# A recurrence feeding a routed expert layer: where a small input check and the first zeroings stand

## The chip, the cores and the metric

The kernel runs on one core of one Trainium2 chip, as one launch. The metric is device time in microseconds (us), the median of several executions. Engines are named as the profile names them: PE (matrix products), DVE, ACT, POOL, and SP, which here only issues DMAs.

## What is computed

Three stages follow each other. The first is a recurrence over 768 tokens for 32 heads (4 batches of 8) with a 40 by 40 state each; the other two are a layer of eight experts, of which every token takes two, and a dense layer.

```python
for t in range(S):                       # S = 768, per batch and head, D = 40
    y[:, :, t] = einsum('bhd,bhde->bhe', rt, state)
    Sa = einsum('bhde,bhe->bhd', state, at)
    state = state * wt[:, :, None, :] - einsum('bhd,bhe->bhde', Sa, bt) + einsum('bhd,bhe->bhde', vt, kt)
...
x = y.transpose(0, 2, 1, 3).reshape(3072, 320)
noisy = x @ w_gate + log1p(exp(x @ w_noise)) * noise      # top 2 of 8 experts, softmax over the two
out[mask] += weight * (relu(x[mask] @ w1[e]) @ w2[e])     # for every expert e and both places
h = out @ w_in; result = maximum(0.01 * h, h) @ w_out
```

## The kernel before

The 768 tokens are cut into 12 chunks of 64 (`NCH`). For each chunk there is a preparation, which needs only inputs, and a chain of steps through the state. The preparation is `load` and `load_w` (DMAs of k with b, of a twice, and of the decays w), `wq` (two scans over the decays, `Dt` and `Et`, for each half q of the heads, their transposes on PE, and the products of k, b and a with them), `sta` and `stk_` (16-bit stacks, transposed by DMA), `ks` (scores on PE) and the steps of a small triangular inverse (`t_load`, `t_step`, `t_fin`). The chain is `c_x`, `c_u`, `c_s`; the outputs are `y_u` to `y_t`, and after each chunk the router's logits are formed. When chunk 11 is near, `Moe.setup` builds the router's constants, `Moe.route` and `Moe.routed` sort the tokens to the experts, and then `moe1` and `moe2` run the two layers.

`Attn.run` gives every step a due number with `at(k, f)`, sorts the steps by it and calls them in that order; the extra steps of the router are in `A.extra` with due numbers of their own. The framework then orders each engine's instructions by its own simulation of the program, so that a moved step can move others with it. Tiles come from pools on two sides of the on-chip memory. A pool that is closed gives its room to later tiles, and the first instruction that writes such a tile waits for the last one that used the room.

What stands at the program's start before: `consts` zeroes the state `S` (L41) and four tiles `x` (L44) on POOL, builds index tiles with `iota` (L47 to L60) and from them masks on DVE (L48 to L62). `body` then takes a pool named `ck`, loads 120 KB of all six inputs (the tile `cx`) by ACT's queue, and finds on DVE whether any of the six is small throughout (L795 to L797, result in `bad`). `Attn.run` opens the pools of the chunks' tiles, which fall on the room of `ck` and of the index tiles, and zeroes on POOL `cd` and `ce` (the scans' second operands), the rows of five tiles `aT` that no load fills, `VU`, `T` and `TT` (all L235). The chunks' loads follow, in the order k with b, a, and so on by chunk (SP's queue is one queue, kept in order). Chunks 0 and 1 have due numbers far below the others.

The second scan of chunk 0, `Et` for q=1, overwrites the only buffer of `Et`, so that it must wait until POOL has multiplied `aT` by the first `Et` (L93).

Of the kernel before, what the change touches and what calls it, by code (L numbers as in the profile page):

```python
# [7 lines left out]
F32 = mybir.dt.float32  # L8
# [10 lines left out]
# head 8g+4f+i is kept as (f, z=4g+i); on the state's rows as (z%2, z//2)  # L19
def host_attn(r,k,v,w,a,b):  # L20
    n=lambda y: np.ascontiguousarray(y.reshape(B,2,4,NCH,C,D).transpose(3,1,4,0,2,5).reshape(NCH,2,C,16*D))       # c f t (z e)
    t=lambda y: np.ascontiguousarray(y.reshape(B,2,2,2,NCH,C,D).transpose(4,3,6,0,2,1,5).reshape(NCH,2,D,16,C))   # c z%2 e (z/2 f) t
    k,b=n(k),n(b); wt=t(w); wz=np.ones((NCH,2,2,64,8,C),np.float32); wz[:,:,:,:D]=wt.reshape(NCH,2,D,2,8,C).transpose(0,3,1,2,4,5); wz[...,0]=0
    wz=np.pad(wz.reshape(NCH,2,128,8*C)[:,:,:104],((0,0),(0,0),(0,0),(1,1)))   # c q (z%2 e) (z/2 f t), without the chunk's first, 0 on both sides
    first=lambda wt: np.ascontiguousarray(np.pad(wt[...,0].transpose(1,2,0,3),((0,0),(0,24),(0,0),(0,0)),constant_values=1).reshape(128,NCH*16)[:104])
    return dict(kb=np.ascontiguousarray(np.stack([np.concatenate([k[:,0],b[:,0]],1),np.concatenate([b[:,1],k[:,1]],1)],1)),
        aa=n(a).reshape(NCH,128,640),rr=n(r).reshape(NCH,128,640),vv=n(v).reshape(NCH,128,640),at=t(a).reshape(NCH,2,D,1024),
        wz=wz,w0=first(wt))

class Attn:  # L30
# [7 lines left out]
    def consts(s,tp):  # L38
        nc=s.nc; cp=s.cp; V=nc.vector; G=nc.gpsimd;
        # state, rows (z%2, e): the first 64 rows' alone, the last 64 rows' alone, all rows'  # L40
        s.S=cp.tile([128,16,120],F32,name="S"); G.memset(s.S,0.0)  # L41
        s.ss=cp.tile([128,16,128],F16,name="ss"); V.memset(s.ss,0.0)
        s.x=[cp.tile([128,4,2,40],F32,name=f"x{i}") for i in range(4)]   # row half f holds f's
        for t in s.x: G.memset(t,0.0)  # L44
        s.VU=[cp.tile([128,2,16,40],F32,name=f"VU{i}") for i in range(2)]
        jp=tp.tile([128,128],I32,name="jp")
        G.iota(jp,pattern=[[1,128]],base=0,channel_multiplier=-1)   # col-row  # L47
        s.idf=cp.tile([128,128],F32,name="idf"); V.tensor_scalar(s.idf,jp,0.0,None,op0=ALU.is_equal)  # L48
        # earlier tokens: of the scores, and of k, b with a (b's rows of the first half against the second half's a)
        s.masky=cp.tile([128,64],F32,name="masky"); s.mask=[cp.tile([128,64],F32,name=f"mask{f}") for f in range(2)]  # L50
        for i in range(2): V.tensor_scalar(s.masky[64*i:64*i+64],jp[64*i:64*i+64,64*i:64*i+64],0.0,2.0**-6,op0=ALU.is_gt,op1=ALU.mult)
        cb=tp.tile([128,64],I32,name="cb"); k=4; nb=4   # nb + col>>k - row>>k
# [8 lines left out]
        s.gap=cp.tile([128,1],F32,name="gap"); t1=tp.tile([128,1],F32,name="t1")   # 0 on the rows between  # L61
        V.tensor_scalar(t1,pr,64.0,2.0**-12,op0=ALU.is_ge,op1=ALU.mult); V.tensor_scalar(s.gap,pr,40.0,2.0**-12,op0=ALU.is_lt,op1=ALU.mult); V.tensor_tensor(s.gap,s.gap,t1,ALU.add)  # L62
        
    # ---- loads of chunk c
    def load_w(s,c,q):
        w=s.K['w',c,q]=s.wp.tile([104,514],F32,name="w",bufs=s.cfg['bw']); s.nc.sync.dma_start(out=w,in_=s.h['wz'][c,q])
    def load(s,c):
        nc=s.nc; K=s.K[c]=dict(); aT=s.aT[c%s.cfg['NA']]
        K['en']=s.st.tile([128,16,40],F32,name="en",bufs=s.cfg['NE']); K['aa']=s.wp.tile([128,16,40],F32,name="aa",bufs=1); K['kb']=[]
        for f in range(2):  # L70
            kb=s.st.tile([128,16,40],F32,name="kb",bufs=s.cfg['NK']); K['kb'].append(kb)
            nc.sync.dma_start(out=kb.rearrange("p a b->p (a b)"),in_=s.h['kb'][c,f])
        nc.sync.dma_start(out=K['aa'].rearrange("p a b->p (a b)"),in_=s.h['aa'][c])
        for p in range(2): nc.sync.dma_start(out=aT[64*p:64*p+40].rearrange("p a b->p (a b)"),in_=s.h['at'][c,p])
    # ---- decays of z 8q..8q+7, and k, b, a with them
    def wq(s,c,q):
# [9 lines left out]
        V.tensor_scalar(w0,W4,2.0**-12,None,op0=ALU.mult)   # the chunk's decay in its first token's place  # L86
# [13 lines left out]
    # rows h,h,l (or h,l,h) of x in a stack, and its transpose  # L100
# [17 lines left out]
    def psx(s,c):   # two banks, [128,4,128] and [128,512]  # L118
        a,b='ys','yy'; f=lambda n,*d: s.ps.tile([128,*d],F32,name=n,bufs=1)
        x=f(a,4,128) if a=='pt' else f(a,8,64).rearrange("p a b->p (a b)").rearrange("p (a b)->p a b",b=128)  # L120
        return x,(f(b,512) if b=='yy' else f(b,8,64).rearrange("p a b->p (a b)"))
# [13 lines left out]
    # ---- T of the diagonal blocks of a group of chunks (two): 32 rows a partition, (chunk, f, z, block)  # L135
# [5 lines left out]
    def blk(s,c,t,off,*d):   # of both blocks of 16  # L141
# [11 lines left out]
    # ---- r, v of chunk c  # L153
# [8 lines left out]
    # ---- chain: heads (f, 4g..4g+3), tokens 32 blk + 16 h..  # L162
# [32 lines left out]
    # ---- y  # L195
    def y_u(s,c,h):   # v's and u's stack of half the heads
# [26 lines left out]
    def y_d(s,c):   # state for the y of chunk c  # L223
# [7 lines left out]
    def run(s):  # L231
# [5 lines left out]
        s.cd=s.wp.tile([104,8,64],F32,name="cd"); s.ce=s.wp.tile([104,8,64],F32,name="ce")  # L237
        zero(s.cd); zero(s.ce); V.memset(s.cd[:,:,63:64],4096.0)
        s.aT=[s.st.tile([128,16,64],F32,name=f"aT{i}") for i in range(F['NA'])]
        for t in s.aT: zero(t[32:64]); zero(t[96:128])  # L240
# [4 lines left out]
        for t in s.VU: zero(t)  # L245
        s.T=s.wk.tile([128,32,32],F32,name="T",bufs=1); zero(s.T)
        s.N=s.wk.tile([128,32,32],F32,name="N",bufs=1); s.tm=s.wk.tile([128,272],F32,name="tmp",bufs=1)
        s.TT=[s.st.tile([128,48,32],F32,name=f"TT{i}") for i in range(2)]; s.nT=0   # k of the first half, zeros, k of the second half
        for t in s.TT: zero(t[:,16:32])
# [7 lines left out]
        last=NCH-1; PC=cf.get('pc',5); dg=PC/4; base=lambda c: PC*c; tl=cf.get('tp',1.)  # L257
        pb=cf.get('pb',0); base=lambda c: PC*c+pb*((c+o)//2); ke=-99
        la=cf.get('la',2.6)   # prep of chunk c goes with the chain of chunk c-la
# [27 lines left out]
RND=6; R=4            # rounds of R token tiles of 128: rows b*768+128*q of round q  # L287
PT=124; NJ=7; CAP=PT*NJ   # slots of an expert: slot p*NJ+j

def tails(w):   # [320,n] -> [128,3,n]: the rows 256.. twice  # L290
    return np.ascontiguousarray(np.stack([w[0:128],w[128:256],np.concatenate([w[256:320],w[256:320]],0)],1))
def gates(w):   # [320,16] -> [128,2,80]: of heads' halves f the first 128 rows; the last 32 rows of batch b's on rows 32b.., columns 16+16b..
# [5 lines left out]
def host_moe(w_gate,w_noise,noise,w1,w2,w_in,w_out):  # L298
    return dict(wgs=gates(np.concatenate([w_gate,w_noise],1)),wg=tails(np.concatenate([w_gate,w_noise],1)),
        noise=np.ascontiguousarray(noise.reshape(4,RND,128,NE).transpose(2,3,1,0)),   # [p, e, round, b]  # L300
# [6 lines left out]
class Moe:  # L307
# [4 lines left out]
    # power of two scale: absmax in [2^k,2^(k+1)) and its inverse; bits worked on in int32 by float arithmetic on exponents  # L312
# [10 lines left out]
    # ---- what routing keeps  # L323
# [10 lines left out]
    def setup0(s,wgs):   # what the logits need  # L334
# [3 lines left out]
    # logits of chunk c: x rows (f, token), [b, 160]  # L338
# [10 lines left out]
    def absmax0(s,z,t):   # part z of the first expert's weights, into t [128,1024]  # L349
# [6 lines left out]
    def setup(s,rk):  # L356
        nc=s.nc; cp=s.P("mcst"); s.rk=rk(); V=nc.vector; G=nc.gpsimd
        with s.tc.tile_pool(name="mtmp",bufs=1) as tp:
# [6 lines left out]
            s.ei=s.rk.tile([128,NE,NTL],F32,name="ei"); G.iota(s.ei,pattern=[[-1,NE],[0,NTL]],base=NE,channel_multiplier=0,allow_small_or_imprecise_dtypes=True)  # 8-e  # L365
# [8 lines left out]
    # am [128,n] -> out [128,2n]: scales, inverses (of the maximum over all partitions)  # L374
# [11 lines left out]
    # exp to float32's accuracy: 2^n exp(f), |f|<=ln2/2; z is lost  # L386
# [15 lines left out]
    # ---- routing of round q: x rows [128,R,320]  # L402
    def big(s): return [s.ra.tile([128,16,40],F32,name="kb",bufs=s.rb).rearrange("p a b->p (a b)") for i in range(2)]
    def direct(s,c,xt):   # rows of chunk c right to where its round is routed
# [24 lines left out]
    def routed(s,q0,q1,nm,E=None,B_=None,A_=None):   # what follows for rounds q0..  # L429
# [10 lines left out]
        # log1p(exp(z)): one step of Newton's from the tables' value  # L440
# [18 lines left out]
        # ranks  # L459
# [11 lines left out]
        # slot p*NJ+j of expert e: its row's place goes to ix[p,e*NJ+j]  # L471
# [13 lines left out]
    def gates(s):   # places in yd and weights of all rows' two experts  # L485
        V=s.nc.vector; S2=lambda m: s.rk.tile([128,2,NTL],F32,name=m,bufs=1); m1,m2=s.m12[:,0],s.m12[:,1]
        t=S2("gt")
        V.tensor_scalar(t,s.r2,float(CAP),1e6,op0=ALU.is_ge,op1=ALU.mult); V.tensor_tensor(t,t,s.r2,ALU.add)   # no room: the last row
# [5 lines left out]
    # ---- weights to hi, lo; returns tiles and inverse scales  # L494
    def wload(s,src,n,name,eng):
        t=s.wf.tile([128,n],F32,name=name); eng.dma_start(out=t,in_=src); return t
    def moe1(s):
# [7 lines left out]
        def prepw(e):   # pieces  # L505
# [30 lines left out]
        def back(left):   # a share of what else has to be done  # L536
# [37 lines left out]
        with s.tc.issue_after(s.hl0.ins), s.tc.issue_after(s.rend.ins):  # L574
            s.after0(); extra=s.w_moe2(s.wk)+s.more(); loadw(1); e0=2
            def low(f):   # not before the next expert's weights are ready
# [9 lines left out]
    # float64's words t[:,1], t[:,0] to float32 in A, 0 below its range  # L586
# [7 lines left out]
    # second experts' weights come as float64: its two words are worked into float32 here  # L594
# [83 lines left out]
def host_slow(r,k,v,w,a,b):   # [t, b*8+h, 6*40]  # L678
    return np.ascontiguousarray(np.concatenate([x.reshape(32,S,40) for x in (r,k,v,w,a,b)],-1).transpose(1,0,2))
class Slow:  # L680
    """everything anew in float32, step by step and with all experts for all tokens"""
# [90 lines left out]
def body(tc,nc,a,cfg={},force=0):  # L772
    RW=cfg.get("rw","tile")
    with ExitStack() as ctx:
# [7 lines left out]
        with ExitStack() as actx:  # L782
# [8 lines left out]
            # scales hold for inputs that aren't small throughout  # L791
            with tc.tile_pool(name="ck",bufs=1) as p:
                x=p.tile([32,4,6,40],F32,name="cx"); mx=p.tile([32,6],F32,name="cm"); V.memset(mx,1.0)
                nc.scalar.dma_start(out=x.rearrange("p t a b->p t (a b)"),in_=a['rk'][0:4].rearrange("t h z->h t z"))
                V.tensor_reduce(mx,x.rearrange("p t a b->p a t b"),axis=AX.XY,op=ALU.max,apply_absolute_value=True)  # L795
                V.tensor_reduce(mx[:,0:1],mx,axis=AX.X,op=ALU.min)
                V.tensor_scalar(bad[0:32,0:1],mx[:,0:1],2.0**-6,None,op0=ALU.is_lt)  # L797
# [31 lines left out]
        def decays():   # the scales hold for decays of up to 1  # L829
# [34 lines left out]
```

## Time and profile before

| what | us |
|---|---|
| median of 3 runs | 1457.26 |
| lowest and highest of them | 1449.39 and 1463.57 |
| span of the profiled execution, first to last instruction | 1467.8 |

The page gives no other time of the profiled execution than its span. The span is 10.5 us above the median of the runs; a difference worked out on the trace is taken over to the median unchanged. Times in rows are us from the span's start. The recurrence takes about the first 600 us, the rest are the two layers.

### The profile page before, as it was taken

How to read it: one execution, taken by the hardware profiler on the slowest of the kernel's cores; microseconds unless marked ns; L12 is line 12 of the kernel's file. 1: busy time of each engine (PE TensorE's matmuls, PEld its weight loads, DVE VectorE, ACT ScalarE, POOL GpSimd, SP SyncE). 2: the span in 40 equal slices, each digit the busy share in tenths (PEclk: the TensorE clock that was granted, in tenths of full speed). 3: DMA queues.
4: the chain of work that ended last, by engine and by line, in shares of the span. 5: the costliest groups of instructions: out<-in, count | busy, mean ns of one | idle time of the engine just before them, and what ended most of it. 6: DMA issues, size and time to landing. Idle time of an engine off the chain costs nothing.

```text
span 1467.8 us, 34853 instructions
## 1 busy us (share of the span) xinstructions
PE 1196.2 (81%) x14439; PEld 896.5 (61%) x14439; DVE 889.6 (61%) x2029; ACT 640.8 (44%) x1535; POOL 489.2 (33%) x559
## 2 busy tenths in 40 slices
PE   1348898898888998338887977979895999999998
PEld 0237687777777887227564755747765555556555
DVE  6797575767775788856544544979633853442321
ACT  1347566666766765303322322434222543533431
POOL 7364424436261443243211202120004443522531
PEclk9997887879998998569988989999997999999999
DMA  7767967799997564678636765655403421110000
GB/s 224 139 129 154 197 128 154 150 175 174 178 174 140 123 151 102 218 109 199 162 99 204 187 202 152 180 157 142 122 32 103 109 68 37 44 30 19 19 19 21
DMA packets 305927, 187.97 MB, mean 128 GB/s; under 512 B 260894, under 2 KB 276355, under 8 KB 304891
## 3 DMA queue, kind: packets, MB, share of 16 engines
q1 hardware_dynamic: 293103, 156.91, 47.6%
q0 software_dynamic: 10368, 16.84, 4.6%
q10 hardware_dynamic: 2288, 11.90, 2.5%
q8 instruction: 115, 1.88, 0.5%
q14 instruction: 53, 0.43, 0.1%
HBM read 105.24 MB, written 23.18 MB: 87 GB/s over the span
## 4 chain that ended last, share of the span: by engine, by line
PE 46%; DVE 20%; DMA 19%; ACT 4%; issue 4%; POOL 4%; SPq 2%; ACTq 0%; DVEq 0%; POOLq 0%
PE ph L660 10%; PE po L670 10%; PE po L564 7%; DMA wf<-w 6%; PE ph L550 5%; PE bk L167 5%; PE bk L179 5%; DVE l L519 2%; DMA w<-wi 2%; DMA nd<-ns 2%; DMA kbt<-stk 1%; DVE wam L509 1%; DMA xr<-xs,ix 1%; DVE kb L99 1%; DMA sd<-ss 1%
## 5 line engine op out<-in xcount | busy, mean ns | idle before, releaser
L550 PE MATMUL ph<-xT,h 128*128 128x372 f16 (+2 forms) x680 | 150.6, 352 | 82.5 <-DVE gl L553 56.7
L552 ACT ACTIVATE gh<-ph 128x372 f16<-128x372 f32 (+2 forms) x136 | 68.0, 509 | 259.8 <-PE ph L550 247.3
L528 POOL DMA_INDIRECT xr<-xs,ix x56 | 83.2, 1485 | 264.7 <-DMA xT<-xr 237.1
L179 PE MATMUL bk<-x,TT 64*32 64x80 f32 x1536 | 153.3, 253 | 9.0 <-ACT x L175 7.0
L550 PEld LDWEIGHTS <-h 128*128 128x128 f16 x680 | 68.3, 101 | 128.6 <-issue 92.5
L664 POOL TENSOR_TENSOR gl<-hc,gh 128x512 f16<-128x512 f32 x80 | 91.9, 1158 | 146.7 <-ACT gh L663 146.5
L179 PEld LDWEIGHTS bk<-x,TT 64*32 64x32 f32 x1536 | 125.6, 137 | 21.5 <-ACT x L175 10.0
L175 ACT ACTIVATE x<-bk 16x160 f32<-16x160 f32 x384 | 113.7, 296 | 57.2 <-PE bk L167 49.2
L181 ACT ACTIVATE VU<-bk 32x160 f32<-32x160 f32 x384 | 112.7, 293 | 58.3 <-PE bk L179 49.7
L564 PE MATMUL po<-h,gl 128*124 128x320 f16 x448 | 134.0, 304 | 2.1 <-DVE wa L514 2.1
L564 PE MATMUL po<-h,gh 128*124 128x320 f16 x448 | 134.9, 303 | 1.0 <-ACT gh L552 0.6
L564 PE MATMUL po<-l,gh 128*124 128x320 f16 x448 | 133.5, 301 | 0.0
L660 PE MATMUL ph<-xT,wih 128*128 128x512 f16 (+2 forms) x560 | 124.7, 353 | 4.9 <-DVE hc L662 1.8
L564 PEld LDWEIGHTS <-gh 128*124 128x124 f16 x896 | 122.3, 137 | 10.2 <-ACT gh L552 1.1
L662 DVE SCALAR_TENSOR_TENSOR hc<-ph,hc 128x512 f32<-128x512 f32 (+2 forms) x112 | 68.3, 612 | 88.7 <-ACT hc L661 88.0
L663 ACT ACTIVATE gh<-hc 128x512 f16<-128x512 f32 (+2 forms) x112 | 62.5, 566 | 120.0 <-PE po L670 66.6
L670 PE MATMUL po<-woh,gh 128*128 128x320 f16 x384 | 113.6, 300 | 0.6 <-DVE y L671 0.5
L167 PE MATMUL bk<-VU,g 128*16 128x40 f32 x3072 | 113.4, 221 | 0.0
L670 PE MATMUL po<-wol,gh 128*128 128x320 f16 x384 | 113.3, 300 | 0.0
L638 POOL DMA_INDIRECT yy<-yd,slot x48 | 48.1, 1001 | 195.1 <-DMA yd<-y 154.8
L670 PE MATMUL po<-woh,gl 128*128 128x320 f16 x384 | 108.9, 300 | 1.1 <-DVE amt L316 0.9
L509 DVE TENSOR_REDUCE wam<-wf 128x1 f32<-128x1024 f32 (+1 forms) x35 | 46.3, 1324 | 102.0 <-DMA wf<-w 101.8
(286 smaller groups left out, 2519.8 us busy)
## 6 DMA issues: line engine op xcount, KB each, us to landing
wf<-w SPq DMA_DIRECT2D x24, 512.0 KB
w<-wi SPq DMA_DIRECT2D x16, 768.0 KB
wf<-w SPq DMA_DIRECT2D x32, 320.0 KB
w<-wo SPq DMA_DIRECT2D x16, 640.0 KB
kb<-kb SPq DMA_DIRECT2D x24, 320.0 KB
yd<-y ACTq DMA_DIRECT2D x7, 1085.0 KB
w<-wz SPq DMA_DIRECT2D x24, 208.8 KB
aa<-aa SPq DMA_DIRECT2D x12, 320.0 KB
```

What stands on the lines that cost most here:

```text
L167: q=64+32*f; nc.tensor.matmul(px[q:q+16,c0:c0+n],l,r,start=st[f],stop=True,skip_group_check=True); st[f]=False
L175: nc.scalar.activation(x[p0+32*f:p0+32*f+16,:,f],px[64+32*f:80+32*f,0:160].rearrange("p (z d)->p z d",d=40),AF.Copy,scale=-0.125)
L179: for z in range(4): nc.tensor.matmul(pu[32:32+n,z],TT[p0:p0+64,16*h:16*h+n,2*(4*g+z)+blk],x[p0:p0+64,z],start=h==0 and z==0,stop=True,ski ...
L181: q=64-64*f+32*blk; nc.scalar.activation(VU[q:q+n,f,4*g:4*g+4],pu[32:32+n,:,f],AF.Copy)
L528: c=e*NJ+j; nc.gpsimd.indirect_dma_start(out=xr[0:PT,j],out_offset=None,in_=s.xs,in_offset=bass.IndirectOffsetOnAxis(ap=s.ix[0:PT,c:c+1],a ...
L550: for n,(t,k,i) in enumerate(ps): nc.tensor.matmul(ph[:,0:N],w(t,k,f),xT[:,j0:j1,i,0:PT],start=n==0,stop=n==7)
L552: nc.scalar.activation(o,ph[:,0:N],AF.Relu)
L564: nc.tensor.matmul(po[0:PT,0:DM],a[:,f,c],b[:,DM*f:DM*f+DM],start=n==0,stop=n==23); n+=1
L660: for n,(t,k,i) in enumerate(ps): nc.tensor.matmul(ph[:,0:N],w(t,k,f),xT[:,b0:b1,i,:],start=n==0,stop=n==7)
L662: nc.vector.scalar_tensor_tensor(c,ph[:,0:N],0.01,c,ALU.mult,ALU.max)
L664: (nc.vector if g<2 else nc.gpsimd).tensor_tensor(gl[:,f,0:N],c,gh[:,f,0:N],ALU.subtract)
L670: nc.tensor.matmul(po[:,0:DM],a[:,f,128*(b-b0):128*(b-b0)+128],bb[:,f,:],start=n==0,stop=n==47); n+=1
```

## The change

The size check becomes a function `small`, put among the extra steps with due number 45.9, just ahead of `setup` (46), and its pool is taken on the other side of the memory. `cd` and `ce` move into the constants' pool and are zeroed first of all. The zeroing of `aT` goes into `load`, once for each of the first five chunks. The zeroing of `VU`, `x`, `S` and `TT` goes into a step `late` with due number -29.05, between the first steps of chunk 0. Comments are dropped, which moves line numbers by two or so.

```diff
     def consts(s,tp):
+        s.cd=cp.tile([104,8,64],F32,name="cd"); s.ce=cp.tile([104,8,64],F32,name="ce")
+        G.memset(s.cd,0.0); G.memset(s.ce,0.0); V.memset(s.cd[:,:,63:64],4096.0)
-        s.S=cp.tile([128,16,120],F32,name="S"); G.memset(s.S,0.0)
+        s.S=cp.tile([128,16,120],F32,name="S")
-        for t in s.x: G.memset(t,0.0)
...
     def load(s,c):
+        if c<s.cfg['NA']: nc.gpsimd.memset(aT[32:64],0.0); nc.gpsimd.memset(aT[96:128],0.0)
...
     def run(s):
-        s.cd=s.wp.tile([104,8,64],F32,name="cd"); s.ce=s.wp.tile([104,8,64],F32,name="ce")
-        zero(s.cd); zero(s.ce); V.memset(s.cd[:,:,63:64],4096.0)
-        for t in s.aT: zero(t[32:64]); zero(t[96:128])
-        for t in s.VU: zero(t)
+        late=lambda: ([zero(t) for t in s.VU+s.x+[s.S]],[zero(t[:,16:32]) for t in s.TT])
-        for t in s.TT: zero(t[:,16:32])
+        at(-29.05,late); last=NCH-1; PC=cf.get('pc',5); dg=PC/4; base=lambda c: PC*c; tl=cf.get('tp',1.)
...
 def body(tc,nc,a,cfg={},force=0):
-            with tc.tile_pool(name="ck",bufs=1) as p:
-                x=p.tile([32,4,6,40],F32,name="cx"); mx=p.tile([32,6],F32,name="cm"); V.memset(mx,1.0)
-                nc.scalar.dma_start(out=x.rearrange("p t a b->p t (a b)"),in_=a['rk'][0:4].rearrange("t h z->h t z"))
-                V.tensor_reduce(mx,x.rearrange("p t a b->p a t b"),axis=AX.XY,op=ALU.max,apply_absolute_value=True)
-                V.tensor_reduce(mx[:,0:1],mx,axis=AX.X,op=ALU.min)
-                V.tensor_scalar(bad[0:32,0:1],mx[:,0:1],2.0**-6,None,op0=ALU.is_lt)
+            def small():
+                with tc.tile_pool(name="ck",bufs=1,side=R_) as p:
+                    x=p.tile([32,4,6,40],F32,name="cx"); mx=p.tile([32,6],F32,name="cm"); V.memset(mx,1.0)
+                    nc.scalar.dma_start(out=x.rearrange("p t a b->p t (a b)"),in_=a['rk'][0:4].rearrange("t h z->h t z"))
+                    V.tensor_reduce(mx,x.rearrange("p t a b->p a t b"),axis=AX.XY,op=ALU.max,apply_absolute_value=True)
+                    V.tensor_reduce(mx[:,0:1],mx,axis=AX.X,op=ALU.min)
+                    V.tensor_scalar(bad[0:32,0:1],mx[:,0:1],2.0**-6,None,op0=ALU.is_lt)
+            A.extra.append((45.9,small))
```

Three places show what the engines' orders make of it. On POOL at the program's start, before, the zeroing of `aT` follows that of `T`:

```order
L235 MEMSET ce 104x512
L235 MEMSET VU_95 128x1280
L235 MEMSET VU_96 128x1280
L235 MEMSET T 128x1024
L140 MEMSET T 64x32x16 x2
L140 MEMSET T 64x2x16 x2
L235 MEMSET aT_160 32x1024 x2
L235 MEMSET aT_161 32x1024 x2
```

and now (the number behind a name is its buffer's; L237 is the old L235, L142 the old L140, L70 the new zeroing in `load`):

```order
L237 MEMSET T 128x1024
L237 MEMSET VU_95 128x1280
L237 MEMSET VU_96 128x1280
L237 MEMSET x_91 128x320
L237 MEMSET x_92 128x320
L237 MEMSET x_93 128x320
L237 MEMSET x_94 128x320
L237 MEMSET S 128x1920
L142 MEMSET T 64x32x16 x2
L70 MEMSET aT_144 32x1024 x2
L237 MEMSET TT_161 128x512
L237 MEMSET TT_162 128x512
```

So `cd`, `ce` and the index tiles come ahead of all this, `x` and `S` have moved behind `VU`, and the same `aT` blocks follow the same amount of zeroing as before, with `TT` now between the first `aT` and the other four.

On SP's queue, from the first loads of v on, before:

```order
L161 DMA VU_95<-vv 64x640 x2
L161 DMA VU_96<-vv 64x640 x2
L66 DMA w<-wz 104x514
L72 DMA kb<-kb 128x640 x2
L74 DMA aT_160<-at 40x1024
L72 DMA kb<-kb 128x640
L74 DMA aT_160<-at 40x1024
L72 DMA kb<-kb 128x640
L74 DMA aT_161<-at 40x1024
```

and now:

```order
L163 DMA VU_95<-vv 64x640
L74 DMA kb<-kb 128x640 x7
L67 DMA w<-wz 104x514
L74 DMA kb<-kb 128x640
L163 DMA VU_95<-vv 64x640
L74 DMA kb<-kb 128x640
L76 DMA aT_144<-at 40x1024
L74 DMA kb<-kb 128x640
L76 DMA aT_144<-at 40x1024
L163 DMA VU_96<-vv 64x640 x2
```

The two halves of chunk 0's `aT` stood behind two and three loads of `kb`, and now stand behind nine and ten, a load of w and one of v.

On DVE at the recurrence's end, before, the router's constants (`onef`, `ones`, `idf` and so on) stood between the 16-bit stack `us` of the outputs and the state's update:

```order
L360 MEMSET onef 2x128
L199 SCALAR_TENSOR_TENSOR us<-VU_95,us 128x16x40
L200 COPY us<-us 128x16x40
L363 MEMSET ones 128x128
L371 MEMSET cnt 128x8
L373 MEMSET fx 128x56
L361 TENSOR_SCALAR idf<-jp 128x128
```

and now the check does, with the state's copy `ss` ahead of it:

```order
L192 SCALAR_TENSOR_TENSOR n_7159<-bk_166,gap,S 104x160
L195 TENSOR_TENSOR S<-n_7159,w_142 40x4x40 x2
L228 SCALAR_TENSOR_TENSOR ss<-S,ss 104x16x40
L229 COPY ss<-ss 104x16x40
L794 TENSOR_REDUCE cm<-cx 32x6
L192 SCALAR_TENSOR_TENSOR n_7366<-bk_163,gap,S 104x160
L795 TENSOR_REDUCE cm<-cm 32x1
L195 TENSOR_TENSOR S<-n_7366,w_142 40x4x40 x2
L796 TENSOR_SCALAR bad<-cm 32x1
L358 MEMSET onef 2x128
```

The reduction of `cx` stands between two updates of the state, and the router's constants and first steps come some ten instructions later than before. Between the start and this place no engine's order has changed.

## Rows read from the trace of the kernel before

**Rows 1.** The page, its first part: span, then each engine's busy time, share and instructions.
```profile
span 1467.8 us, 34853 instructions
...
PE 1196.2 (81%) x14439; PEld 896.5 (61%) x14439; DVE 889.6 (61%) x2029; ACT 640.8 (44%) x1535; POOL 489.2 (33%) x559
```
**Rows 2.** Busy time of each engine in stretches: length, PE, PEld, DVE, ACT, POOL, clock, DMA share, GB/s.
```profile
15.00:27.00 12.00, 1.56 (x8) 0.92 (x6) 5.06 (x11) 1.60 (x2) 11.45 (x13) 1.00 0.92 266
27.00:60.00 33.00, 10.00 (x92) 7.25 (x92) 26.65 (x50) 9.72 (x21) 16.58 (x11) 1.00 0.74 174
60.00:110.00 50.00, 23.76 (x254) 19.01 (x254) 44.84 (x100) 20.34 (x53) 26.05 (x29) 0.98 0.68 131
490.00:510.00 20.00, 16.79 (x472) 14.81 (x469) 16.16 (x50) 15.15 (x46) 13.12 (x33) 1.00 0.65 133
```
**Rows 3.** The chain that ended last, 0 to 115 us: start, length, what.
```profile
10.03 2.27 DMA cx<-rk
...
14.93 0.95 POOL aT L235
...
24.92 0.99 POOL TT L235 x2
25.91 1.24 POOL aT L93
27.17 1.24 DVE Et L88
```
**Rows 4.** Timeline of POOL, 0 to 62 us: start, length, engine, instruction, idle before.
```profile
8.49 1.50 POOL L140 MEMSET T<- 64x512 f32 x4
14.93 9.93 POOL L235 MEMSET aT<- 32x1024 f32 x10 [4.94 <-DVE bad L797]
```
**Rows 5.** Timeline of all engines, 4.3 to 5 and 5 to 6 us.
```profile
4.39 3.15 DVE L51 TENSOR_SCALAR masky<-jp 64x64 f32<-64x64 int32 x1
4.76 0.52 POOL L235 MEMSET ce<- 104x512 f32 x1
...
5.23 2.27 POOL L235 MEMSET VU<- 128x1280 f32 x2
```
**Rows 6.** Timeline of DVE, 0 to 62 us.
```profile
9.79 0.14 DVE L62 TENSOR_TENSOR gap<-gap,t 128x1 f32<-128x1 f32 x1
...
12.32 1.14 DVE L795 TENSOR_REDUCE cm<-cx 32x6 f32<-32x960 f32 x1
...
14.52 0.12 DVE L796 TENSOR_REDUCE cm<-cm 32x1 f32<-32x6 f32 x1
14.68 0.14 DVE L797 TENSOR_SCALAR bad<-cm 32x1 f32<-32x1 f32 x1
...
21.08 0.81 DVE L86 TENSOR_SCALAR w<-W 104x8 f32<-104x8 f32 x1
```
**Rows 7.** Timeline of SP's queue, 0 to 60 us.
```profile
15.04 0.83 SPq L72 DMA_DIRECT2D kb<-kb  x2
15.93 0.35 SPq L74 DMA_DIRECT2D aT<-at  x1
```
**Rows 8.** DMA issues, 0 to 60 us: tile, queue, count, KB each.
```profile
kb<-kb SPq DMA_DIRECT2D x10, 320.0 KB
aT<-at SPq DMA_DIRECT2D x12, 160.0 KB
w<-wz SPq DMA_DIRECT2D x6, 208.8 KB
...
VU<-vv SPq DMA_DIRECT2D x4, 160.0 KB
```
**Rows 9.** Timeline of ACT, 470 to 500 us.
```profile
489.34 1.85 ACT L175 ACTIVATE x<-bk 16x160 f32<-16x160 f32 x6
...
494.95 0.72 ACT L225 ACTIVATE ss<-S 104x640 f16<-104x640 f32 x1
```
**Rows 10.** The chain that ended last, 470 to 510 us.
```profile
490.62 6.21 DMA ut<-us
```

More of the change, by code (lines that the diff above doesn't have):

```diff
@@ L38, in consts @@
     def consts(s,tp):
-        nc=s.nc; cp=s.cp; V=nc.vector; G=nc.gpsimd;
-        s.S=cp.tile([128,16,120],F32,name="S"); G.memset(s.S,0.0)
+        nc=s.nc; cp=s.cp; V=nc.vector; G=nc.gpsimd
+        s.cd=cp.tile([104,8,64],F32,name="cd"); s.ce=cp.tile([104,8,64],F32,name="ce")
+        G.memset(s.cd,0.0); G.memset(s.ce,0.0); V.memset(s.cd[:,:,63:64],4096.0)
+        s.S=cp.tile([128,16,120],F32,name="S")
         s.ss=cp.tile([128,16,128],F16,name="ss"); V.memset(s.ss,0.0)
         s.x=[cp.tile([128,4,2,40],F32,name=f"x{i}") for i in range(4)]
-        for t in s.x: G.memset(t,0.0)
         s.VU=[cp.tile([128,2,16,40],F32,name=f"VU{i}") for i in range(2)]
@@ L256, in at @@
         def at(k,f,*a): it.append((k,len(it),f,a))
-        last=NCH-1; PC=cf.get('pc',5); dg=PC/4; base=lambda c: PC*c; tl=cf.get('tp',1.)
+        at(-29.05,late); last=NCH-1; PC=cf.get('pc',5); dg=PC/4; base=lambda c: PC*c; tl=cf.get('tp',1.)
         pb=cf.get('pb',0); base=lambda c: PC*c+pb*((c+o)//2); ke=-99
```

## The prediction

> **What bounds the kernel now.** I read the page first: a span of 1467.8 us in which DVE is busy 61% [rows 1], so no engine bounds the whole, and the change must be priced where it acts: the first 30 us and the end of the recurrence. Then the chain of waits over the start [rows 3]. There the reader sees the load of `cx` (2.27 us), then the zeroing of `aT`, ten blocks from 14.93 on, then `TT`, then POOL's product `aT` by `Et`, and only then, at 27.17, DVE's second `Et` scan. The timeline of POOL says the same from the engine's side [rows 4]: it stood idle 4.94 us until DVE had written `bad`, because `aT` lies on the room of the check's tiles. For the same reason SP issued the first `kb` at 15.04 [rows 7], some 5.2 us after the last mask (9.79 plus 0.14 [rows 6]). From 27 us on DVE is the busiest engine, 26.65 of 33 us and then 44.84 of 50 [rows 2], so what brings the second `Et` forward is passed on to the first steps of the chain at about 110 us, and through it to the recurrence. The orders shown with the change differ nowhere between the start and the recurrence's end.
>
> **What goes at the start.** The check's wait goes. What then holds the `aT` zeroing is the same amount of zeroing as before (the sets ahead of it differ only by the two smallest pieces of `T`) and the masks, whose index tiles lie under `aT` and `kb`. So I must ask when the masks are done. In the trace the second `masky` took 3.15 us, from 4.39 to 7.54 [rows 5], an operation over 64 elements a row; POOL was zeroing back to back. Later, `w<-W` took 0.81 us for 8 elements a row [rows 6] while POOL zeroed `aT` [rows 4]. So a one-input operation of DVE is held while POOL zeroes. In the changed order POOL runs `T`, two `VU`, four `x`, `S` and two blocks of `T` without a pause, the same work that ended at about 9.6 us before (the four pieces of `T` run from 8.49 to 9.99 [rows 4], the last two are short). I therefore expect the masks to be done at about 9.8 us, hardly earlier than before, though their index tiles stand behind less, and the first scan to start where it did. Earliest is 4 to 5 us, if DVE gets in at once; latest about 10.3.
>
> The Trainium skill (SBUF — State Buffer, "Who interferes with whom") says that a DVE operation in a two-port mode and a POOL operation exclude each other for a whole instruction, and that whichever issues first holds the ports. Read simply, DVE would then get in at the end of POOL's current instruction. The 0.81 us agree; the 3.15 us do not, since DVE was passed over at the end of `ce` and of the first `VU` [rows 5]. By that rule the masks would be done at about 5 us, and the result is the first rival.
>
> **What the start is worth.** Two things can hold the second `Et` after the change, and the later one decides.
> - POOL alone: `aT` starts at 9.8 in place of 14.93, 5.1 us sooner; ten blocks, `TT` and the two small pieces of `T` (0.35 us, now behind them) follow. Its product would start at 25.9 - 5.1 + 0.35 = 21.1.
> - The load of chunk 0's `aT`. Its second half stands behind ten `kb`, one w and one v, so 3200 + 208.8 + 160 + 320 = 3889 KB, 3.98 MB, must land [rows 8]. At the 266 GB/s of 15 to 27 us [rows 2] that is 15.0 us from the first issue at 9.8: it lands at 24.8. Before, the two halves stood behind only two and three `kb`, and POOL was late, not the load.
>
> So the product starts at 24.8 instead of 25.9, a gain of 1.1 us where POOL alone would have given 4.8. The cover that is gone here is the interleaving of the loads. If the first bytes take 2.3 us more, as `cx` did [rows 3], it starts at 27.1, a loss of 1.2. Between -4.8 and +1.2 I take -1.1, by the rate that the same loads had. The DMA queues also empty earlier, since the same loads start 5.2 us sooner; the transposes behind them wait mostly for DVE, and I give that -0.5 (bounds 0 and -2).
>
> `cd` and `ce` first, and `S`, `x`, `VU`, `TT` later, cost nothing: these are the same instructions on POOL, hidden behind the loads, and the state is first needed near 110 us. Without that cover `S` and the four `x` would cost their 2.9 us of POOL. The other zeroings of `aT` wait for no load; the loads wait for them, and stand behind `kb` anyway.
>
> **What the end costs.** DVE's three instructions (1.14, 0.12 and 0.14 us [rows 6]) come into a stretch where it is busy 16.16 of 20 us [rows 2], and ACT issues one DMA more. Behind the reduction on DVE wait the next update of the state, then the router's constants. In the changed order ACT issues `cx` where the `x` copies of 489.34 stood [rows 9], and the data would be there about 2.3 us later. DVE comes to the reduction after `ss`: on ACT three pairs of `x` (1.85), `ss` (0.72) [rows 9], then about 1.15 on DVE, so nearly 4 us later. No wait, then, unless the load is slow: a transpose there took 6.21 us [rows 10]. The 1.4 us count fully only where DVE is the chain, and I take half, +0.7. Bounds: +1.4 and a wait of 2.5 us and the issue make about +5; against that, `ss` is pulled ahead of the router's first steps, from 494.95 [rows 9] to about 491.5, which could give up to 3.4 us back.
>
> **Sum** on the profiled execution: -1.1 - 0.5 + 0.7 = -0.9, so 1467.8 becomes 1466.9. Its span stands 10.5 us above the median of the runs; taken over to that median, 1457.3 - 0.9 = 1456.4. I predict 1456 us, no change that the runs could show: about 1% (14.6 us) is what a measurement of this kernel can tell from none, and its runs lie 14 us apart.
>
> **Rivals.**
> - *The masks get in early.* For it: only `cd` and `ce`, half a microsecond each [rows 5], stand ahead of the index tiles now, and the 0.81 us row; against it: the 3.15 us row. Then `kb` starts near 5 us, the `aT` data are there by 20, POOL's 21.1 decides, -4.8, and the emptier queues give their full -2: 1467.8 - 6.8 + 0.7, on the median about 1451.
> - *The loads' order takes it all back.* For it: ten `kb` ahead of one `aT`; against it: `kb` spreads over 128 rows and may move faster than the mix did. At +1.2 and +0.7, without the half us of the queues: 1459.
> - *Slower: the late check holds the recurrence.* The place is DVE at about 493 us, in order; the price is the wait for `cx` and then the reduction, with the update of the state behind it, and the router's steps pushed into 500 to 560 us, where DVE is full. It decides once `cx` takes more than the 4 us of slack; at 6.2 us the whole +5 counts, and the start's -1.6 goes off it: 1461. For it: every transpose and scattered store in that stretch. Against it: DMA is not full there, 0.65 [rows 2].
> - *The change does not do what it says.* The check could still stand in the start's way, were its tiles under others; the orders show `cx` on ACT's queue only at the recurrence's end, so I give that nothing.
>
> **How the numbers follow.** The forecast 0.5, with 1453 to 1460 as its own range; early masks 0.18; loads' order 0.14; late check 0.18. None of these cases reaches 1%. What does is that the order of some 300 DVE instructions at the recurrence's end has changed, and that the median of a few runs scatters by some 5 us. For that I leave 0.10 on the faster side, where two of the cases lie, and 0.07 on the slower, 0.83 within 1%. The range goes past the outer cases, 1451 and 1461, by that scatter: 1446 to 1467.
>
> **What would show it.** In the changed profile: `bad` is gone from the start; the last mask (`gap`, `mask`) ends at 9 to 10.3 us and `kb` is issued right behind it (early masks: at 5); POOL zeroes `aT` from about 9.8 on; its first product waits for a DMA and starts at 23.5 to 26.5 (21 if POOL decides); the second `Et` starts 1.26 us later, against 27.17. At the recurrence's end DVE's wait ahead of the reduction is under 1 us. I am wrong if the second `Et` stands before 23 us and the whole gains more than that, or if the stretch from 490 to 640 us is longer by more than 5 us.

## The result

| | before | after |
|---|---|---|
| median of 19 runs each, taken in turn, us | 1460.1 | 1473.7 |
| lowest and highest of them | 1437.7 and 1475.4 | 1457.0 and 1494.1 |
| ratio after/before, 95% interval | | 1.0127 [1.0088, 1.0167] |
| span of the profiled execution | 1467.8 | 1463.1 |

The change made the kernel slower by about 1.3%; no change was forecast. Disturbed runs are left out of the ratios, here and below, so that these are not quotients of the medians; the profiles of e6 and e7 below are of such runs. The two profiled executions mislead if one compares their spans: that of after is one of its quicker runs, that of before one of its longer ones. What can be compared is a stretch between two events that both have. Two such stretches carry the result: the start, and the 160 us from the recurrence's last chunks to the first product of the expert layer.

**The start.** The chain of waits of after, up to the second `Et`; it answers to [rows 3]:

```profile
2.34 6.12 DVE masky L52
...
12.88 7.06 DMA kb<-kb
...
20.00 8.80 DMA aT<-at
...
28.98 1.27 POOL aT L95
...
30.27 1.24 DVE Et L90
```

The load of `cx` and `bad` are gone from the chain, as expected. In their place stand one mask of 6.12 us and two DMA waits. The second `Et` is at 30.27 where it was at 27.17: the start lost 3.1 us. DVE's timeline gives the masks (columns: start, duration, engine, line, operation):

```profile
2.34 6.64 DVE L52 TENSOR_SCALAR masky<-jp 64x64 f32<-64x64 int32 x2
...
10.17 0.39 DVE L60 TENSOR_SCALAR mask<-cb 64x64 f32<-64x64 int32 x2
...
30.27 1.22 DVE L90 TENSOR_TENSOR_SCAN Et<-w,ce 104x512 f32<-104x512 f32 x1 [7.24 <-POOL aT L95]
```

and POOL's timeline, against [rows 4], why:

```profile
2.33 0.95 POOL L237 MEMSET T<- 128x1024 f32 x1
3.22 2.27 POOL L237 MEMSET VU<- 128x1280 f32 x2
5.44 1.28 POOL L237 MEMSET x<- 128x320 f32 x4
6.66 1.70 POOL L237 MEMSET S<- 128x1920 f32 x1
...
10.69 1.94 POOL L70 MEMSET aT<- 32x1024 f32 x2 [1.19 <-DVE mask L60]
...
28.98 1.26 POOL L95 TENSOR_TENSOR aT<-aT,Et 104x512 f32<-104x512 f32 x1 [6.87 <-DMA aT<-at]
```

The first `masky` was held from 2.34 to 8.46, past the ends of `T`, both `VU`, all four `x` and `S`; the last mask ended at 10.56. Then POOL zeroed, and stood still for 6.87 us until the load of `aT` had landed. SP's queue, to be held against [rows 7]:

```profile
10.59 3.19 SPq L74 DMA_DIRECT2D kb<-kb  x7
...
17.99 0.31 SPq L76 DMA_DIRECT2D aT<-at  x1
18.77 0.33 SPq L74 DMA_DIRECT2D kb<-kb  x1
20.00 0.31 SPq L76 DMA_DIRECT2D aT<-at  x1
21.59 1.86 SPq L163 DMA_DIRECT2D VU<-vv  x2
23.75 6.53 SPq L76 DMA_DIRECT2D aT<-at  x8
```

and the window from the first `kb` to the landing of that `aT` (columns as in [rows 2]: length, then busy time of PE, its weight loads, DVE, ACT and POOL, granted clock, DMA share, GB/s):

```profile
10.59:28.81 18.22, 1.91 (x8) 1.27 (x8) 8.19 (x19) 1.72 (x2) 10.76 (x14) 1.00 0.89 253
```

**The recurrence's end.** As boundaries I take the 37th update of the state, and the first product of the expert layer. Before, DVE's timeline at the first of them:

```profile
494.75 0.37 DVE L190 SCALAR_TENSOR_TENSOR n<-bk,gap,S 104x160 f32<-104x160 f32 x1
```

PE's timeline at the second:

```profile
643.39 1.19 PE L550 MATMUL ph<-xT,h 128*128 128x248 f16 x5 [14.74 <-DMA xT<-xr]
```

and the window between them:

```profile
494.80:643.40 148.60, 95.05 (x2154) 81.64 (x2149) 122.65 (x424) 70.36 (x195) 59.43 (x69) 0.77 0.58 140
```

After, the same three; the check's reduction stands just ahead of the first boundary on DVE:

```profile
483.36 0.32 DVE L229 COPY ss<-ss 104x640 f16<-104x640 f16 x1
483.59 1.13 DVE L794 TENSOR_REDUCE cm<-cx 32x6 f32<-32x960 f32 x1
484.66 0.36 DVE L192 SCALAR_TENSOR_TENSOR n<-bk,gap,S 104x160 f32<-104x160 f32 x1
```

The second boundary, on PE:

```profile
644.26 0.99 PE L548 MATMUL ph<-xT,h 128*128 128x248 f16 x4 [16.00 <-DMA xT<-xr]
```

The window:

```profile
484.70:644.30 159.60, 105.55 (x2152) 91.31 (x2145) 122.78 (x439) 71.11 (x196) 62.96 (x76) 0.69 0.54 131
```

The reduction follows the copy of `ss` without a gap: DVE waited for no `cx`. But the stretch is 11 us longer (159.6 against 148.6), with the same number of products within the trace's few missing ones, and DVE and ACT as busy as before (122.8 and 71.1 us against 122.7 and 70.4). What grew is PE's busy time, by 10.5 us, and what fell is the granted clock, from 0.77 to 0.69. One group of the stretch's instructions by forms shows it (count, busy us, mean ns, idle before), first in before:

```profile
L179 PE MATMUL bk<-x,TT 64*32 64x80 f32 x312 | 27.6, 236 | 0.8 <-ACT x L175 0.8
```

and in after:

```profile
L181 PE MATMUL bk<-x,TT 64*32 64x80 f32 x312 | 34.0, 261 | 2.2 <-ACT x L177 2.2
```

The same 312 products took 34.0 us in place of 27.6. Windows of 10 us place part of it. The first boundary comes 10.1 us earlier in after, so that its windows from 500 and 560 stand against those from 510 and 570 before. Before:

```profile
510.00:520.00 10.00, 9.87 (x270) 9.05 (x266) 9.85 (x28) 7.86 (x24) 3.40 (x5) 1.00 0.54 110
570.00:580.00 10.00, 8.53 (x222) 7.21 (x221) 6.67 (x22) 5.40 (x19) 5.27 (x6) 1.00 0.48 123
```

After:

```profile
500.00:510.00 10.00, 9.46 (x121) 8.84 (x123) 8.66 (x26) 3.69 (x12) 3.49 (x8) 0.55 0.68 138
560.00:570.00 10.00, 9.39 (x150) 8.37 (x151) 3.77 (x14) 4.75 (x16) 2.98 (x3) 0.67 0.40 87
```

At the first place PE finished 270 products at a granted clock of 1.00 (the 2.4 GHz level) before, and 121 at 0.55 (nearly all of the window at 1.2 GHz) in after, busy over 94% both times. At the second it was 222 at 1.00 and 150 at 0.67.

One pair of profiles cannot carry this alone. From the first to the 37th update, where the orders are the same, the window was, before,

```profile
125.93:494.75 368.82, 322.29 (x7165) 280.14 (x7161) 255.18 (x566) 244.56 (x710) 145.64 (x222) 0.85 0.83 162
```

and after

```profile
129.08:484.66 355.58, 312.80 (x7182) 271.50 (x7178) 255.92 (x556) 243.88 (x710) 144.04 (x217) 0.88 0.88 168
```

It was 13.2 us shorter in after, at a higher clock, though nothing was changed there; over all twelve profiles it takes 355 to 374 us. The clock of a stretch scatters that much from run to run, so that the loss must be shown by many runs and by other kernels.

### The profile page after: what moved, and what is told of

Its sections match the earlier page's. It is cut to its first block, busy times and chain, and to the rows that moved or that the text cites. A ratio compares the mean times of both kernels' runs of the same rounds, so it can differ in the third digit from the quotient of the medians.

```text
span 1463.1 us, 34852 instructions
## 1 busy us (share of the span) xinstructions
PE 1195.9 (82%) x14439; PEld 896.6 (61%) x14439; DVE 892.1 (61%) x2029; ACT 641.0 (44%) x1535; POOL 489.7 (33%) x559
## 4 chain that ended last, share of the span: by engine, by line
PE 50%; DVE 19%; DMA 18%; ACT 4%; issue 4%; POOL 3%; SPq 2%; ACTq 0%; DVEq 0%; POOLq 0%
PE ph L658 10%; PE po L668 10%; PE po L562 8%; DMA wf<-w 7%; PE ph L548 6%; PE bk L181 6%; PE bk L169 5%; DVE l L517 2%; DMA kbt<-stk 2%; DVE wam L507 1%; DVE kb L101 1%; ACT x L177 1%; DVE Dt L84 1%; DMA nd<-ns 1%; DMA ut<-us 1%
## 5 line engine op out<-in xcount | busy, mean ns | idle before, releaser
L181 PE MATMUL bk<-x,TT 64*32 64x80 f32 x1536 | 157.0, 255 | 10.8 <-ACT x L177 9.3
```

The lines of the kernel that those rows point to most:

```text
L181: for z in range(4): nc.tensor.matmul(pu[32:32+n,z],TT[p0:p0+64,16*h:16*h+n,2*(4*g+z)+blk],x[p0:p0+64,z],start=h==0 and z==0,stop=True,ski ...
```

## The experiments

Three theories stood at the outset. A: the new order at the recurrence's end costs the time. B: the start costs it. C: the granted clock carries the difference. From e4 on, A means that the new order leaves TensorE longer at its lower level. Each kernel ran 12 times, the kernel before 23 to 35 times beside it (medians 1461.4, 1461.5 and 1455.6 on the three chips used: the first for the change again and e1 to e3, the second for e4 to e7, the third for e8 and e9). A difference between two medians of 12 runs is uncertain by some 8 us (95%, by redrawing the runs). The column "second Et" and the stretch (37th update to first product) are from the one profile of each; the clock is the mean granted clock over all runs.

| kernel | second Et | order at the end | clock | stretch | median | ratio to before, 95% |
|---|---|---|---|---|---|---|
| before | 27.2 | before's | 0.909 to 0.912 | 148.6 | 1461 | |
| the change again | 29.6 | new | 0.900 | 158.4 | 1471.7 | 1.0077 [1.0034, 1.0121] |
| e1: late check alone | 26.6 | new | 0.900 | 164.4 | 1468.2 | 1.0082 [1.0043, 1.0122] |
| e2: new start alone | 27.9 | before's | 0.911 | 158.1 | 1461.9 | 0.9975 [0.9927, 1.0023] |
| e3: check in layer | 29.9 | before's | 0.908 | 144.1 | 1468.1 | 1.0063 [1.0026, 1.0101] |
| e4: before, check in layer | 26.6 | before's | 0.912 | 146.9 | 1460.3 | 1.0005 [0.9949, 1.0061] |
| e5: index tiles right | 22.7 | new | 0.903 | 158.9 | 1463.4 | 1.0053 [1.0005, 1.0102] |
| e6: e3 and e5 | 22.7 | before's | 0.910 | 155.7 | 1458.1 | 1.0021 [0.9980, 1.0063] |
| e7: check at 57 | 29.2 | third | 0.910 | 155.3 | 1465.9 | 1.0043 [0.9996, 1.0091] |
| e8: check at start, right | 27.9 | before's | 0.909 | 143.9 | 1464.8 | 1.0050 [1.0015, 1.0085] |
| e9: e5 and e7 | 22.7 | third | 0.908 | 154.5 | 1458.4 | 1.0046 [1.0011, 1.0081] |

The mean clock of the changed kernel's first 19 runs is 0.901. Within the runs of any one of these kernels, where the order is the same, the time falls by 9 to 15 us per 0.01 of mean clock (11 to 12 in the runs of before).

The check's place at the recurrence's end was taken back in three kernels that differ from their partner in nothing else: from the change again to e3 (3.6 us), from e5 to e6 (5.3) and from e1 to e4 (7.9). Each difference is no larger than its uncertainty, but all have one sign. A least-squares fit to all 213 runs behind the table (a level for each chip, a term each for the new and the third order, and one per us of second `Et`) gives 8 us for the new order (95%: 5 to 12) and about 1 us per us of second `Et` (0.3 to 1.6). For the clock it gives 0.0085 less for the new order (0.006 to 0.011), and nothing for the second `Et`.

**The change again.**

> The changed kernel once more, on the chip of the three runs beside it. If the slowdown is the kernel's own and not a chance of the first runs, the ratio to before is again near 1.013, some 18 us. If it was chance, the ratio is within 0.5% of 1.

10 us over before at a clock of 0.900 against 0.909: the loss repeats, somewhat smaller. The ratio, 1.0077, lies between the two that were expected.

**e1, the late check alone.** The kernel before, with `small` as an extra step:

```diff
+            def small():
+                with tc.tile_pool(name="ck",bufs=1,side=R_) as p:
...
+            A.extra.append((45.9,small))
```

> Before, with only the check moved to due number 45.9; the zeroings stay where they were. The instruction orders of PE and ACT are then the changed kernel's from start to end, so the recurrence's end is the changed one; the start is a third one (aT's zeroing early, loads of kb ahead of aT). Theory A, the recurrence's end costs the time: 10 us or more above before, a ratio of 1.007 to 1.013. Theory B, the start costs it (the second Et scan came 3.1 us later and the whole recurrence runs on from there): within 0.3% of before unless its second Et is late as well. Theory C, neither place but the granted clock of TensorE: a lower mean clock than before's runs and a time that goes with it.

The start is 0.5 us better than before, and yet the kernel is 0.8% slower, at the changed kernel's clock. The start cannot be the main cause.

**e2, the new start alone.** The changed kernel with the check back at the program's start, in its old room:

```diff
-            A.extra.append((45.9,small))
+            with tc.tile_pool(name="ck",bufs=1) as p:
...
```

> The changed kernel with the check put back at the start, in its old room; only the zeroings are moved. The orders at the recurrence's end are then those of before. Theory A (the end): equal to before, ratio 0.997 to 1.003. Theory B (the start): the second Et scan stands where before had it or later, and the ratio follows it by at most 3 us, 1.002. Theory C (clock): no forecast but that time and clock go together.

Time and clock are those of before. Without the late check, the moved zeroing is neither gain nor loss.

**e3, the check in the expert layer.** The changed kernel, with `small` among the layer's background work. `small` itself now takes the room of `cx` from the layer's pool and loads it by SP's queue.

```diff
...
-            A.extra.append((45.9,small))
+            m.small=small
...
-        m.more=lambda: [finite]+decays()+[verdict]; m.moe1()
+        m.more=lambda: [finite]+decays()+[m.small]+[verdict]; m.moe1()
```

> The changed kernel with the check moved on, out of the recurrence's end and into the expert layer's background work. The start is the changed kernel's (second Et scan at about 30 us), the recurrence's end is that of before. Theory A (the end): 3 us above before, ratio about 1.002, and 12 to 15 us under the changed kernel. Theory B (the start): as slow as the changed kernel, 1.010 to 1.014.

The clock came back to 0.908, and 3 to 4 us of the time with it, no more, where theory A expected 12 to 15: a miss. The start of this kernel is the changed one (second `Et` at 29.9). So either the start costs more than its 3 us, or the check costs time in the layer too, or 12 runs were too few. The next kernel separates the first two.

**e4, the same in the kernel before.** `small` is that of e3.

```diff
...
-        m.more=lambda: [finite]+decays()+[verdict]; m.moe1()
+        m.more=lambda: [finite]+decays()+[m.small]+[verdict]; m.moe1()
```

> The kernel before with only the check moved, not to the recurrence's end but into the expert layer, between the decays' checks and the verdict. Its order at the recurrence's end is that of before on PE, ACT and DVE; at the start, POOL zeroes aT early, and eight loads of kb stand ahead of the first aT, as in the run with the late check alone. Theory A (the changed order at the recurrence's end leaves TensorE at its lower level for longer): the mean granted clock is that of before, 0.907 to 0.911, the late check alone had 0.900; the time is within 4 us of before, some 6 to 10 us under the late check alone. Theory B (the start decides): the time is that of the late check alone, about 1468. Theory D (the small check costs time wherever it stands late): 1465 or more at a clock of 0.907 to 0.911.

Equal to before, at the highest clock of all: the check in the layer costs nothing that can be seen. e1 and e4 have the same start (second `Et` at 26.64 in both profiles), each was run beside a median of before that agrees within 0.1 us, and they differ by 7.9 us and by 0.012 of clock. That pair differs by the late check alone (the ratios' intervals just overlap). e3 against e4 has the two starts with before's order: 3.3 us of second `Et` and 7.8 us of time, so that the start, or the scatter of 12 runs, is worth more there than the trace says.

**e5, the start alone undone.** The changed kernel with the index tiles on the other side of the memory, so that `kb` and `aT` do not lie on their room. PE, ACT and DVE have the changed kernel's order throughout:

```diff
-        with s.tc.tile_pool(name="actmp",bufs=1) as tp: s.consts(tp)
+        with s.tc.tile_pool(name="actmp",bufs=1,side="right") as tp: s.consts(tp)
```

> The changed kernel with one word more: the pool of the index tiles, under the masks, is taken on the other side of the memory, so that kb and aT no longer lie on its room. The orders of PE, ACT and DVE are those of the changed kernel; on SP the loads of kb come first and the first aT stands behind three and four of them; POOL zeroes the first aT right behind T. Expected at the start: kb issued within 4 us, the first product of POOL at 13 to 19 in place of 28.98, the second scan at 14 to 20, and the first update of the state 8 to 14 us earlier than 129. Theory A (start worth +3, recurrence's end the rest): the clock stays at 0.898 to 0.902, the time is the changed kernel's 1472 less the gain at the start, 1460 to 1464, equal to before. Theory B (the start alone made the change slower): well below before, 1450. A third: the gain at the start is not passed on through the recurrence: 1468 or more.

8.3 us faster than the changed kernel by the medians, at nearly its clock: theory A with its price of the start. At the start itself three expectations were missed: the product came at 20.78 (13 to 19 expected), the second `Et` at 22.71 (14 to 20), and the first update at 121.3 in place of 129.1, 7.8 us earlier (8 to 14). The stretch at the end stayed long. POOL's timeline of this kernel:

```profile
3.34 1.94 POOL L70 MEMSET aT<- 32x1024 f32 x2
...
20.78 1.26 POOL L95 TENSOR_TENSOR aT<-aT,Et 104x512 f32<-104x512 f32 x1
```

and DVE's:

```profile
2.34 1.99 DVE L52 TENSOR_SCALAR masky<-jp 64x64 f32<-64x64 int32 x2
...
9.74 1.84 DVE L86 COPY w<-w 104x8 f32<-104x8 f32 x1
...
22.71 1.23 DVE L90 TENSOR_TENSOR_SCAN Et<-w,ce 104x512 f32<-104x512 f32 x1
```

The product no longer waits for a load, but for POOL's own zeroing. The two `masky` took 1.99 us here and 6.64 in the changed kernel, with another zeroing beside them.

**e6, both undone.** e3 and e5 together.

> The changed kernel with both its losses taken away: the check stands in the expert layer, so that the order at the recurrence's end is that of before, and the index tiles are on the other side of the memory, so that the first loads wait for nothing. Theory A: clock 0.907 to 0.911 and 8 to 14 us under the same kernel with the index tiles under aT (1468): 1454 to 1460, faster than before by 2 to 8. If the gain at the start is not passed on: 1465 to 1469.

10 us under e3, from the start alone, which was worth 7.2 us at the second `Et` (3.6 at the first update). It is the lowest median beside 1461.5 of before, but its ratio to before is 1.0021 [0.9980, 1.0063]: no version found is shown to beat before.

**e7, the check later.** The changed kernel with one number changed:

```diff
-            A.extra.append((45.9,small))
+            A.extra.append((57,small))
```

> The changed kernel with one number changed: the check's due number is 57 in place of 45.9, behind the router's constants. The start is the changed kernel's. At the recurrence's end DVE's constants of the router come first again, as before, then the check's instructions, and PE's order differs from both kernels at some 1100 of 12700 places. Theory A, if any order that is not that of before costs clock: 0.898 to 0.902 and 1470 to 1475. If it is the place ahead of the router's constants that costs clock: 0.907 to 0.911 and 1465 to 1468 (the start's +3 stays). Theory B (the start decides): 1472, at the changed kernel's clock or not.

The clock and the 1465.9 us are those forecast for "the place ahead of the router's constants". The one profile agrees only by half: its stretch is 155.3 us long, but it is of the slowest of the twelve runs (1474.4 us).

**e8, the check at the start in room of its own.** e5 with the check at the start, its pool `ck` on the other side too.

> The changed kernel with the check back at the start, but with the check's tiles and the index tiles both on the other side of the memory. The order at the recurrence's end is that of before. On SP the first five loads of kb and an aT now stand ahead of the first w, which the first scan needs, so that the first scan comes later than 13.6. Theory A (order at the end sets the clock, a gain at the start is passed on): clock 0.907 to 0.912; first scans at 15 to 18, the second one at 19 to 25, some 3 to 8 us before the 27.17 of before; the time 1454 to 1459, 3 to 8 under before. If the start's gain is not passed on: 1460 to 1463.

A miss: 1454 to 1459 us were expected. The chain of its start shows why the start won nothing:

```profile
4.66 6.72 DMA kb<-kb
11.39 6.20 DMA rr<-rr
...
19.83 1.23 DVE Et L90
```

With the room free, seven `kb` and two `aT` were issued ahead of the two w that the first scan needs (five and one were expected ahead of them); the first `Et` stands at 19.83 (13.77 in the changed kernel), the second at 27.86, and the gain at `aT` is spent. It does not explain the loss: the second `Et` and the first update (125.91 against 125.93) stand as in before, the order at the recurrence's end is that of before, and the kernel is 0.5% slower. Some 3 us go with the clock, 0.909 against 0.912; the rest is open. Its orders differ from before's in the layers too, from about 636 us on, but so do those of e4, which is not slower.

**e9, e7 with the index tiles moved.**

> The changed kernel with the check at due number 57 and the index tiles on the other side of the memory. PE, ACT and DVE have the order of the run with the check at 57 but for a few places in the dense layer. Theory A: clock 0.908 to 0.912, and 6 to 8 us under the run with the check at 57 alone (1465.9): 1458 to 1460. If the clock of that order was chance: 0.899 to 0.903 and 1464 to 1468.

The median and the clock are those forecast, but the kernel before was quicker on this chip too, so that the ratio did not move, and the 6 to 8 us under e7 do not show in it. With the runs of each kernel brought to a clock of 0.905 by the line through its own runs, e9 is at 1462.7 and e7 at 1470.1, 7.4 us apart (before 1466.2 and 1465.6 beside them).

## Why the prediction was wrong

- **The masks.** Forecast 9.8, latest 10.3; measured 10.56. The mechanism, DVE held by POOL's zeroing, was right, the hold of one `masky` (6.12 us) twice as long as the 3.15 us of [rows 5].
- **The load of aT: the term that was mis-sized at the start.** Forecast 24.8, at the latest 27.1; measured 28.81 by the chain (20.00 and 8.80). Three things make up the 4.0 us: the first issue 0.8 later; 3.98 MB at 253 GB/s (the window's rate) in place of 266, 15.7 us for 15.0; and the rest of the 4.61 MB that moved in those 18.22 us. That rest, 0.63 MB, is 2.5 us: the `VU` and `aT` issued at 21.59 and 23.75 do not wait until the load ahead of them has landed. I had counted only the bytes ahead of the load in the queue. So the start was +3.1 at the second `Et`, not -1.1. The rival that the loads' order takes it back had the mechanism, at too low a price: 1.2 where it cost 3.1.
- **The queues emptying earlier, -0.5.** Nothing of it is seen: the first update of the state is at 129.08 against 125.93, 3.15 us later, as the second `Et` was 3.10 later (2.56 and 2.46 in the repeat; in e3, with the same start, only 0.5 and 2.75).
- **The late check, +0.7: the step that failed.** As a wait and a work load on DVE it was right: no wait for `cx`, 1.4 us of instructions. But it was priced as work on DVE alone ("the 1.4 us count fully only where DVE is the chain"), and the sum has no term for TensorE's clock, though PE is the busiest engine there, 16.79 of 20 us [rows 2]. The prediction did name the new order of some 300 DVE instructions as a risk, without a mechanism, and gave 0.07 to a loss of over 1% from it. What the runs showed in its place: with the order that came with the check PE stands at the lower of its two levels for longer. The three pairs give 3.6, 5.3 and 7.9 us for it, the fit to all runs 8, and the change's two series, 0.008 to 0.009 of clock at some 12 us per 0.01, give 10.
- **The sum.** 3 from the start and 8 to 10 from the clock, against 13.6 between the medians (10.3 in the repeat). Brought to a clock of 0.905 by the line through its own runs, the changed kernel is at 1468.9 and 1466.7 (the repeat), before beside the repeat at 1466.7: at an equal clock 0 to 2 us are left. In the prediction's own working, the wait from the last mask to the first `kb` is 5.1 us and not 5.2, and 1.4, 2.5 and an issue (0.35 us on ACT in after) make 4.3 and not "about +5"; neither moved the forecast.
- **The other rivals.** Early masks: no, 10.56. The late check holding the recurrence by a slow `cx`: its place was right, its mechanism was not, since `cx` was there in time. The test that I had set, a stretch from 490 to 640 longer by over 5 us, is met: 11 us, though by one pair of profiles.

Open is why this order lowers the clock. All four series with the new order have a mean of 0.900 to 0.903; before and the seven others have 0.908 to 0.912. In the stretch the four profiles with the new order have a granted clock of 0.67 to 0.69 and last 158 to 164 us. The six with before's order have 0.70 to 0.79 and 144 to 158 us, e7 and e9 0.73 and 0.74 and 155 us; e2, with 158.1 us, comes close to the new ones, so that the order makes a long stretch likelier rather than fixing it. The difference between the means over the stretch, 0.07 over some 160 us, accounts for nearly all of the 0.0085 over the whole run.

The profiles also show where it begins, which is the sharpest mark of the new order. In all four with the new order the clock falls 16 to 18 us behind the 37th update and stays at 1.2 GHz for 10 to 14 us (501.1 to 511.3 in after). With before's order no fall starts there in any of six; of the two with the third order it does in e9 (at 18.5, for 6.8 us). What comes ahead of it differs as regularly. In the 5 us before the 37th update PE is busy for 4.1 us with 110 to 116 products in the eight other profiles, before's line being

```profile
489.75:494.75 5.00, 4.12 (x110) 3.74 (x105) 2.99 (x18) 4.74 (x13) 2.69 (x9) 1.00 0.84 213
```

and for the whole 5 us with 146 to 149 products in the four with the new order, after's being

```profile
479.66:484.66 5.00, 5.00 (x149) 4.60 (x143) 3.85 (x9) 4.67 (x15) 1.88 (x7) 1.00 1.03 236
```

PE lost a short pause there. Whether that makes the clock fall is not shown. That the clock costs the time, and not the reverse, is argued from the rows: the same products take longer while DVE and ACT do the same. No kernel set the clock by itself.

## What to carry to other kernels

A wait that is taken off the start gives back only what the next one leaves; for a load, count all that is in flight until it lands, behind it in the queue too, and look at which loads the scheduler will send first once their room is free. A small step put into a dense, scheduler-ordered stretch is priced by the new order, not by its instructions: compare the mean granted clock over many runs, and one stretch between two events in several profiles, before believing a span. Where tiles lie on the room of scratch tiles, moving the scratch to the other side can be worth more than moving the work (8 us in e5 and 10 in e6; nothing in e8, where other loads then went first).

## What the runs showed that was not expected

- A DVE operation with one input can be passed over by POOL several times in a row: 6.12 us for `masky` of 64 elements a row, past the ends of eight zeroings. The Trainium skill (SBUF — State Buffer, "Who interferes with whom") says that a DVE operation in a two-port mode and a POOL operation exclude each other, and that whichever issues first has the ports for the whole instruction. In the changed kernel the hold was that of a whole row of POOL's instructions; no run shows in which mode `masky` ran. In e5, where `aT` follows `T`, the rule fits: the two `masky` took 1.05 and 0.91 us, each about as long as the one zeroing beside it (0.95).
- The mean granted clock of one and the same kernel ranges from 0.885 to 0.924 over the runs of before beside the experiments, and the time with it, from 1441.6 to 1491.9 us.
